# Four attention units ahead of the chunks instead of eight, queries of the last eight units turned on VectorE, and a stacked low-rank product

## Chip, cores and metric

One core of one Trainium2 chip runs the whole program in one launch. The metric is the device time in microseconds (us) of an execution; lower is better. The engines are TensorE (PE), VectorE (DVE), ScalarE (ACT), GpSimd (POOL) and SyncE (SP), which here only issues DMAs.

## What is computed

An attention in two steps feeds a gated channel mixer, which feeds a low-rank token mixer with a second two-layer channel mixer. All arrays are fp32.

```python
p_packed = sm_attn(p, k, v)            # 8 batches x 8 heads, 32 packed queries, 576 tokens, 64 dims
x = sm_attn(q, p_packed, p_packed)     # -> (8, 576, 512)
xk, xr = mu_k*x + (1-mu_k)*x_prev, mu_r*x + (1-mu_r)*x_prev
x = sigmoid(xr @ w_r) * (relu(xk @ w_k)**2 @ w_v)          # w_r 512x512, w_k 512x1024, w_v 1024x512
u = x + (x.transpose(0,2,1) @ U @ V).transpose(0,2,1)      # rank 32, U 576x32, V 32x576
out = u + relu(u @ w_ch1) @ w_ch2                          # 512x2048, 2048x512
```

## The kernel before, in words

**Plan and order.** Nothing is issued where it is written. Each helper of `Plan` records an operation with its tiles, and `emit` (L341) then plays the program with a small cost model (delays between engines `LAT`, a DMA that costs SP 60 ns, 500 ns of gap, its bytes at a fixed rate and 1700 ns to land) and takes, engine by engine, the ready operation with the lowest class `cls` and the lowest number. What comes out is one fixed order for each engine, so a different cost in the model is a different program. All DMAs go out from SP, but for the `wb` loads of phase 2, which go out from POOL.

**Attention** (`attention_steps`, L648). 16 units, one for each pair of batches (bp = 0..3) and pair of heads (j = 0..3). A unit loads `kin`, `qin`, `vin`, turns k and q on PE against an identity (`psat<-ident,qin`, nine 128x128 transposes in three groups, then copies out of PSUM into `qt`), makes the packed keys, and writes `xo` to `x_d` in HBM. Units 0 to 7 are "plain" (fp32 products without splitting, `NPLAIN`); 8 to 15 use split operands. Before, units 0 to 7 run as the **lead** (`NLEAD = 2*NJ`) on four sets of buffers (`A0`, B, C, D), each used twice.

**Weights.** `Cast` (L866) loads fp32 rows into `st` tiles and splits them into a high and a low fp32r part with four TENSOR_SCALAR and three SCALAR_TENSOR_TENSOR instructions on DVE. w_r and half of w_k are cast in the lead, the other twelve (`LATER`: all of w_v and the second half of w_k) once the lanes' buffers are free, in `cast_late` (L1003).

**Chunks.** Twelve chunks of 384 tokens, three for each pair of batches. A chunk loads x (`load_x`, L1043), mixes it with its shifted self, and runs `r_block` (psr, 36 matmuls of 512 columns), `k_block` (psk, 96 of 384), `v_block` (psv, 72 of 512), `x2_out` and `xu_block` (psu). Before, chunks 0 and 1 run interleaved, with x, r and kk of both in `A0`'s buffers (`x_lead`, `r_lead`, `kk_lead`, `xin_lead`). The attention of units 8 to 15 is laid between the chunks from chunk 2 on, `w_ch1` and `w_ch2` are split and stored to HBM from chunk 2, and `make_ws` (L1208) builds the weight sums of phase 2 in chunks 10 and 11.

**Phase 2.** Nine quarters of 512 tokens, eight f steps each: `product` (L1319) makes the seven products of a Strassen step (`psc<-ob,wb`, 256 columns), `c2_block` (L1342) the second layer (`psc<-w,hid`, 512 columns). The next quarter's u is loaded (`load_u`, L1252), gets the low-rank term (`h_block`, L1260: two matmuls psh for each tile of 128 tokens, since `vst` holds a high and a low part padded with zeros) and is turned (`t_block`).

Of the kernel before, what the change touches and what calls it, by code (L numbers as in the profile page):

```python
# [100 lines left out]
class Plan:  # L101
# [234 lines left out]
    TICK = 10240.0 / 3.0  # L336

# [3 lines left out]
    def emit(self):  # L341
# [27 lines left out]
        def release(op):  # L369
            def ready_on(e):  # L370
                return max([p.fin + self.lag(p.eng, e) for p in op.preds], default=0.0)
# [37 lines left out]
        while True:  # L409
# [46 lines left out]
            if op.cost == "dma":  # L456
                clock[e] = t + (60.0 if e == "sp" else 1000.0)
                dge = max(dge, t + 60.0) + 500.0
                wire = max(wire, dge + 700.0) + dur
                op.fin = wire + 1700.0  # L460
            else:
# [9 lines left out]
                clock[e] = t + dur  # L471
# [6 lines left out]
def packed_attention_moe_mixer_kernel(  # L478
# [31 lines left out]
    LANES, ORDER = "BCD", (0, 1, 2, 3, 0, 1, 2, 3)  # L510
# [66 lines left out]
    class Bufs:  # L577
# [24 lines left out]
        def tile_in(self, tag):  # L602
            return plan.tile(self.big_p, [P, 1152], F32, "big", parts=(0, 1, 2, 3), name=tag)
# [44 lines left out]
    def attention_steps(A, u, u_next):  # L648
# [69 lines left out]
        for c in range(3):  # L718
            yield
            ps = ps_att()  # L720
            for t in range(3):
                i = 3 * c + t
                plan.transpose(ps[:, t * P:(t + 1) * P], qin[:, i * P:(i + 1) * P], ident)
            n = 3 if c < 2 or not plain else 2
            w = 8 if plain else NI
            plan.copy(
                qt[:, 0:w * P].rearrange("p (b i c) -> p i b c", b=2, i=w)[:, 3 * c:3 * c + n],
                ps[:, 0:n * P].rearrange("p (i c b) -> p i b c", i=n, b=2))
            if c == 2 and plain:
# [194 lines left out]
    es_w1, es_att, es_x, es_st = ExitStack(), ExitStack(), ExitStack(), ExitStack()  # L924
# [7 lines left out]
    cv = Cast(es_att, "right")  # L932
# [4 lines left out]
    lane = [AX_[i] for i in ORDER]  # L937
    nxt = {}
    for u in range(NLEAD):
        nxt[u] = next((w for w in range(u + 1, NLEAD) if lane[w] is lane[u]), None)  # L940

# [10 lines left out]
    for what in FIRST.split():  # L952
# [8 lines left out]
        else:  # L961
            {"k": lane[u].load_k, "q": lane[u].load_q, "v": lane[u].load_v}[what[0]](u, go)
# [7 lines left out]
    steps = [attention_steps(lane[u], u, nxt[u]) for u in range(NLEAD)]  # L970
    prev = {w: u for u, w in nxt.items()}
    step = 0
    while any(s is not None for s in steps):
        if steps[NJ - 1] is None:
            att_banks[0] = banks[0:3] + banks[5:8]
        for i, s in enumerate(steps):
            if s is None or step < i * LAG or (i in prev and steps[prev[i]] is not None):
                continue
            if next(s, False) is False:
# [4 lines left out]
    rs = [plan.tile(A0.big_p, [P, 1152], F32, "big", parts=(0, 1), name="rs") for _ in range(3)]  # L984
    r_lead = [t.at(h)[:, h * 512:(h + 1) * 512] for t in rs for h in range(2)]
    pairs = [plan.tile(A0.big_p, [P, 1152], F32R, "big", parts=(0, 1), name="prs")[:, 0:2 * CW]
             .rearrange("p (a c) -> p a c", a=2) for _ in range(5)]
    x_lead, kk_lead = pairs[0:2], pairs[2:5]
    xin_lead = [t.vt.bitcast(F32)[:, 0:1024].rearrange("p (j c) -> p j c", j=2) for t in kk_lead[1:3]]
# [53 lines left out]
    def load_x(n):  # L1043
        b, c = chunks[n]
        if n == 1:
            for h, t in enumerate(xin_lead):
                plan.dma(t, x_d[b].rearrange("(j p) n -> p j n", p=P)[:, 2 * h:2 * h + 2, c * CW - P:c * CW + CW], cls=0)
            xin[n] = lambda j: xin_lead[j // 2][:, j % 2]
            return
# [25 lines left out]
    def r_block(n, t):  # L1075
# [7 lines left out]
        r = r_lead.pop(0) if r_lead else plan.tile(r_p, [P, 512], F32, "r")  # L1083
# [7 lines left out]
    def k_block(n, m):  # L1091
# [11 lines left out]
        if n < 2 and (2 * m + n) % 6 < 3:  # L1103
            kk = kk_lead[(2 * m + n) % 3]
        else:
            kk = plan.tile(kk_p, [P, 2, CW], F32R, "kk", parts=(0, 1))
# [3 lines left out]
    def v_block(n, m):  # L1110
        if m == 0:
            vps[n] = [plan.bank(banks[5 + t:6 + t] if n == 1 else ps_v, "psv", n != 1) for t in range(3)]
# [41 lines left out]
    vx_p, st_p, u_p, wb_p, w2r_p, tr_p = rpools = [Pool(bufs=n) for n in (1, 5, 4, 11, 1, 3)]  # L1154

    def open_r():
        es_att.close()
        for n, pl in zip("vx st2 u wb w2r tr".split(), rpools):
# [12 lines left out]
    c2_tags = [(home[t], t) for t in ["wk2_1", "wk3_1"] + [f"wv{m}" for m in range(MK)]]  # L1171
    c2_tags += [(w2r_p, "c2_0"), (w2r_p, "c2_1"), (xs_p, "xs")]
# [17 lines left out]
    def make_v():  # L1190
        vst = plan.tile(vx_p, [P, 2, NI, 2, 64], F32R, "vst", parts=(0, 1))
        vst_.append(vst)
        for c in range(2):
# [3 lines left out]
            for i0, i1 in ((0, 5), (5, NI)):  # L1197
                s = plan.tile(st_p, [P, 512], F32, "s", name="s_v")
                sv = s[:, 0:(i1 - i0) * 64].rearrange("p (i b c) -> p i b c", b=2, c=32)
                plan.zero(sv)  # L1200
                for g in range(4):
                    gr = slice(g * 32, (g + 1) * 32)
                    plan.copy(sv[gr, :, g % 2, :],
# [363 lines left out]
```

## Time and profile before

| | |
|---|---|
| median of 3 runs (lowest to highest) | 1488.79 us (1486.19 to 1491.61) |
| the profiled execution: its time, its span | 1491.34 us, 1489.6 us |
| granted TensorE clock, mean | 0.983 of 2.4 GHz |
| PE busy | 1461.4 us, 98% |
| PE weight loads (beside PE) | 1277.7 us, 86% |
| DVE busy | 980.2 us, 66% |
| ACT busy | 728.3 us, 49% |
| POOL busy | 270.3 us, 18% |
| chain that ended last | PE 92%, DMA 3%, DVE 2%, SP's queue 1% |
| HBM read, written | 229.84 MB, 60.89 MB |

The stages follow each other in time: the lead up to about 92 us, where the first psr stands, chunks up to about 700 us, and phase 2 behind that. Busy shares are means over all three. A matmul's duration in the rows overlaps that of the next one, so what a matmul holds PE for is read from one start to the next.

### The profile page before, as it was taken

What the parts mean: (1) busy time and instruction counts of PE and PEld (TensorE: products, weight loads), DVE (VectorE), ACT (ScalarE), POOL (GpSimd) and SP (SyncE); (2) the same over time, 40 slices, a digit from 0 to 9 for tenths busy, and PEclk for the clock granted to TensorE, in tenths of its full rate; (3) what the DMA queues carried; (4) which work ended last, traced back from release to release, by engine and by line L of the source; (5) the groups of instructions that cost most, each with busy time, mean ns of one, the idle gap of its engine ahead of it and who ended that gap; (6) DMA issues with size and microseconds to landing.
All of it is one profiled execution on the core that took longest, in us unless ns stands there. A gap on an engine that the chain in (4) does not pass through costs nothing.

```text
span 1489.6 us, 25587 instructions
## 1 busy us (share of the span) xinstructions
PE 1461.4 (98%) x9208; PEld 1277.7 (86%) x9208; DVE 980.2 (66%) x2143; ACT 728.3 (49%) x1534; POOL 270.3 (18%) x522
## 2 busy tenths in 40 slices
PE   6999999999999999999999999999999999999998
PEld 5667888888888888889899999899999999999997
DVE  6677877788888888786855464545555555554533
ACT  5567656666666666676533233323333332333332
POOL 0000000000000000001333333333333333333331
PEclk9689999999999999999999999999999999999999
DMA  8863335654655446666988888888888878878763
GB/s 233 234 175 121 114 101 137 205 182 136 186 179 156 141 141 218 207 226 191 314 228 237 211 208 245 198 244 229 231 212 229 213 201 239 213 216 222 206 176 99
DMA packets 213708, 292.42 MB, mean 196 GB/s; under 512 B 70224, under 2 KB 105360, under 8 KB 213584
## 3 DMA queue, kind: packets, MB, share of 16 engines
q1 hardware_dynamic: 141008, 158.65, 34.7%
q0 software_dynamic: 72576, 132.15, 34.0%
q8 instruction: 74, 1.21, 0.3%
q14 instruction: 50, 0.41, 0.1%
HBM read 229.84 MB, written 60.89 MB: 195 GB/s over the span
## 4 chain that ended last, share of the span: by engine, by line
PE 92%; DMA 3%; DVE 2%; SPq 1%; ACT 1%; issue 1%; DVEq 0%
PE psc L197 50%; PE psk L197 13%; PE psv L197 12%; PE psr L197 7%; PE psat L197 5%; PE psat L209 3%; SPq L319 1%; PE psh L197 1%; PE psu L197 1%; DMA kin<-in_k_dram 1%; DMA s<-w_d 1%; DMA qin<-in_q_dram 0%; DMA x_d<-xo 0%; DMA prs<-x_d 0%; DVE ob L254 0%
## 5 line engine op out<-in xcount | busy, mean ns | idle before, releaser
L197 PE MATMUL psc<-w,hid 128*128 128x512 f32 x1728 | 420.7, 391 | 0.2 <-ACT xu L288 0.2
L197 PEld LDWEIGHTS psc<-ob,wb 128*128 128x128 f32 x3024 | 386.4, 191 | 15.1 <-ACT tmp L288 0.8
L197 PE MATMUL psc<-ob,wb 128*128 128x256 f32 x3024 | 391.1, 282 | 0.4 <-ACT tmp L288 0.4
L319 POOL DMA_DIRECT2D wb<-ws_d x504 | 267.3, 530 | 565.5 <-PE psc L197 436.9
L197 PEld LDWEIGHTS psc<-w,hid 128*128 128x128 f32 x1728 | 314.9, 188 | 60.7 <-DVE hid L273 0.7
L233 ACT ACTIVATE hid<-tmp 128x256 fp32r<-128x256 f32 x216 | 131.6, 676 | 229.8 <-DVE tmp L254 229.8
L197 PE MATMUL psk<-xk,wk 128*128 128x384 f32 x1056 | 208.4, 340 | 1.3 <-ACT sq L233 0.8
L197 PE MATMUL psv<-wv,kk 128*128 128x512 f32 x783 | 202.0, 395 | 0.0
L197 PEld LDWEIGHTS psk<-xk,wk 128*128 128x128 f32 x1056 | 184.6, 188 | 10.6 <-issue 1.5
L197 PEld LDWEIGHTS psv<-wv,kk 128*128 128x128 f32 x783 | 144.2, 188 | 28.3 <-issue 0.8
L273 DVE SCALAR_TENSOR_TENSOR hid<-tmp,hid 128x256 fp32r<-128x256 f32 x216 | 126.5, 631 | 49.8 <-ACT hid L233 48.3
L254 DVE TENSOR_TENSOR tmp<-tmp,psc 128x256 f32<-128x256 f32 x288 | 113.1, 410 | 64.4 <-PE psc L197 64.1
L273 DVE SCALAR_TENSOR_TENSOR hid<-psc,hid 128x256 fp32r<-128x256 f32 x72 | 45.3, 629 | 166.5 <-ACT hid L233 166.5
L233 ACT ACTIVATE hid<-psc 128x256 fp32r<-128x256 f32 x72 | 45.9, 637 | 147.9 <-PE psc L197 147.5
L197 PE MATMUL psr<-wr,xr 128*128 128x512 f32 x414 | 112.3, 404 | 0.1
L311 POOL MEMSET x<- 128x8 f32 x4 | 0.5, 113 | 538.4 <-DVE m L270 538.1
L197 PEld LDWEIGHTS psr<-wr,xr 128*128 128x128 f32 x414 | 75.8, 190 | 18.4 <-issue 3.2
L288 ACT ACTIVATE tmp<-psc 128x256 f32<-128x256 f32 x144 | 56.5, 392 | 54.1 <-PE psc L197 53.5
L233 ACT ACTIVATE sq<-psk 128x384 f32<-128x384 f32 x96 | 46.5, 490 | 66.0 <-PE psk L197 63.6
L254 DVE TENSOR_TENSOR kk<-sq,kk 128x384 fp32r<-128x384 f32 x87 | 47.8, 552 | 32.0 <-ACT kk L288 31.8
L270 DVE SCALAR_TENSOR_TENSOR m<-x,mu_t,m 128x384 f32<-128x384 f32 x88 | 51.6, 610 | 0.9 <-ACT m L233 0.9
L233 ACT ACTIVATE m<-x,om_t 128x384 f32<-128x384 f32 x88 | 50.8, 607 | 2.5 <-DVE xr L254 1.8
(176 smaller groups left out, 1645.9 us busy)
## 6 DMA issues: line engine op xcount, KB each, us to landing
wb<-ws_d POOLq DMA_DIRECT2D x504, 256.0 KB, 3.7
st<-in_moe_w_ch_dram SPq DMA_DIRECT2D x32, 512.0 KB, 5.3
ws_d<-wb SPq DMA_DIRECT2D x56, 256.0 KB, 3.0
qin<-in_q_dram SPq DMA_DIRECT2D x32, 288.0 KB, 5.7
x_d<-xo SPq DMA_DIRECT2D x16, 576.0 KB, 3.4
x_d<-x SPq DMA_DIRECT2D x36, 256.0 KB, 2.2
u<-x_d SPq DMA_DIRECT2D x36, 256.0 KB, 5.2
out_dram<-u SPq DMA_DIRECT2D x36, 256.0 KB, 3.2
```

The costliest lines, as they stand in the source:

```text
L197: self.nc.tensor.matmul(o, l, r, start=start, stop=stop, **k)
L209: self.nc.tensor.transpose(out.get(), in_.get(), ident.get())
L233: self.nc.scalar.activation(o, in_.get(), func, **k)
L254: return self.elem(engs, lambda e, o, x, y: e.tensor_tensor(out=o, in0=x, in1=y, op=op), out, [a, b], self.TT, cls)
L270: ("dve",), lambda e, o, x, y, z: e.scalar_tensor_tensor(out=o, in0=x, scalar=z, in1=y, op0=op0, op1=op1), out, [a, b, s], {"dve": (1.042, ...
L273: ("dve",), lambda e, o, x, y: e.scalar_tensor_tensor(out=o, in0=x, scalar=s, in1=y, op0=op0, op1=op1), out, [a, b], self.TT, cls)
L288: self.nc.scalar.activation(o, i, AF.Copy)
L311: (self.nc.gpsimd if eng == "pool" else self.nc.vector).memset(o, 0.0)
L319: (self.nc.sync if eng == "sp" else self.nc.gpsimd).dma_start(out=o, in_=i)
```

## The change

Four things at once, and the planner's model beside them.

- **Lead and chunks.** `NLEAD = NJ`: units 0 to 3 run ahead, one for each set of buffers. The chunks go one by one from 0, and the attention of the next pair of batches (units 4 to 7, then 8 to 11, then 12 to 15) is laid over the three chunks of the pair before.
- **Queries of units 8 to 15** come in by eight DMAs of 32 partitions, with runs of 32 elements, and are turned in 32x32 blocks by two STREAM_TRANSPOSE instructions on DVE (`plan.turn`) instead of nine PE transposes and copies.
- **Conversion buffers** stay open behind the casts and become homes of three `w2` tiles and of `u` tiles; `make_ws` runs in chunks 7 to 10, all of `w_ch1` is cast ahead of `w_ch2`.
- **Low-rank product.** `vst` has no padding, X is stacked by batch, and a tile takes one psh matmul (two for the ninth). For this, u and the output move in halves of 64 rows, and xu in pieces of 32 rows.
- **Planner.** DMA costs have two settings, and DVE and ACT instructions that follow one another early in the program are taken to overlap.

```diff
+    AHEAD = 110000.0
+    CHUNKS = 500000.0
+    OVER = {"act": 100.0, "dve": 83.0}
+    LEAD = (60.0, 500.0, 1.0, 1700.0)
+    LOADED = (300.0, 100.0, 1.19, 3000.0)
...
-                clock[e] = t + (60.0 if e == "sp" else 1000.0)
-                dge = max(dge, t + 60.0) + 500.0
-                wire = max(wire, dge + 700.0) + dur
-                op.fin = wire + 1700.0
+                issue, gap, share, land = self.LEAD if t < self.CHUNKS else self.LOADED
+                clock[e] = t + (issue if e == "sp" else 1000.0)
+                dge = max(dge, t + issue) + gap
+                wire = max(wire, dge + 700.0) + dur * share
+                op.fin = wire + land
...
-    NLEAD = 2 * NJ
+    NLEAD = NJ
-    NPLAIN = 8
+    NPLAIN = 2 * NJ
...
+            if u >= NPLAIN:
+                for b2 in range(2):
+                    for h in range(2):
+                        src = q[2 * bp + b2, 2 * j + h].rearrange("(r t) (e s) -> e r t s", t=2 * NI, e=2)
+                        for e in range(2):
+                            g = 2 * h + e
+                            plan.dma(t.at(2 * g + b2)[g * 32:(g + 1) * 32, b2 * S:(b2 + 1) * S]
+                                     .rearrange("p (t s) -> p t s", s=32), src[e], after=after)
+                return
...
-        for c in range(3):
+        for c in range(3 if plain else 0):
...
+        if not plain:
+            yield
+            for b2 in range(2):
+                r = slice(b2 * S, (b2 + 1) * S)
+                plan.turn(qt[:, r].rearrange("p (i r e) -> p e i r", i=NI, e=2), qin[:, r])
...
-    steps = [attention_steps(lane[u], u, nxt[u]) for u in range(NLEAD)]
+    steps = [attention_steps(AX_[u], u, NJ if u == 0 else None) for u in range(NLEAD)]
...
-    for n in range(2, len(chunks)):
+    for n in range(len(chunks)):
         b, c = chunks[n]
-        if c == 2 and b + 2 < NBP:
+        if c == 0 and b + 1 < NBP:
             plan.cls = 1 if b == 0 else 0
-            for u in range((b + 2) * NJ, (b + 3) * NJ):
+            for u in range((b + 1) * NJ, (b + 2) * NJ):
                 attention(A0, u, u + 1 if u + 1 < NU else None)
...
-        for a in range(2):
-            plan.mm(ps, vst_[0].at(a)[:, a, i].rearrange("p b c -> p (b c)"), xt[b], start=(a == 0), stop=(a == 1))
+        if t < NI - 1:
+            k2 = t % 4
+            plan.mm(ps, vst_[0][:, 2 * k2:2 * k2 + 2].rearrange("p e c -> p (e c)"), xt[b, t // 4],
+                    start=True, stop=True)
+        else:
+            for b2 in range(2):
+                plan.mm(ps, vst_[0][:, NI - 1 + 2 * b2:NI + 1 + 2 * b2].rearrange("p e c -> p (e c)"), xt[b, b2],
+                        start=(b2 == 0), stop=(b2 == 1))
...
-                plan.dma(dst[:, i, :], u)
+                for to, i, rows in hs:
+                    plan.dma(dst[rows, i, :], u[to])
```

Over the whole program PE goes from 8562 to 8458 instructions (72 q transposes and 32 psh matmuls fewer), DVE from 2145 to 2134, ACT stays at 1472, POOL goes from 527 to 524, and SP from 623 to 782 (u and out from 36 each to 68, q from 32 to 80, xu pieces from 16 to 64).

SP's queue in the second half of the lead, before and now. `kin_261`, `qin_262` and `vin_326` are unit 4's (set `A0`), `kin_755` is the second unit of another set, `x_d0_65<-xo` the store of a finished unit, `x_233<-x_d0_65` a piece of chunk 0's x, and `st` a weight to be cast.

```order
L319 DMA x_d0_65<-xo_445 128x1152
L319 DMA st_725<-in_moe_w_k_dram 128x1024
L319 DMA kin_755<-in_k_dram 128x2x256 x2
L319 DMA kin_755<-in_k_dram 64x2x64 x2
L319 DMA x_233<-x_d0_65 128x384
L319 DMA x_233<-x_d0_65 128x2x63
L319 DMA st_815<-in_moe_w_k_dram 128x1024
L319 DMA kin_261<-in_k_dram 128x2x256 x2
L319 DMA kin_261<-in_k_dram 64x2x64 x2
L319 DMA qin_262<-in_q_dram 64x18x64 x2
```

```order
L319 DMA x_d0_65<-xo_448 128x1152
L319 DMA st_705<-in_moe_w_k_dram 128x1024
L319 DMA st_797<-in_moe_w_k_dram 128x1024
L319 DMA kin_261<-in_k_dram 128x2x256 x2
L319 DMA kin_261<-in_k_dram 64x2x64 x2
L319 DMA qin_262<-in_q_dram 64x18x64 x2
L319 DMA vin_326<-in_v_dram 128x2x256
L319 DMA vin_326<-in_v_dram 64x2x64
L319 DMA vin_326<-in_v_dram 128x2x256
L319 DMA vin_326<-in_v_dram 64x2x64
```

Before, the second units of all four sets are loaded here (`kin_755` is one of them); now unit 4 alone is, and the pieces of x and of weights that stood among those loads move up.

PE around unit 4's q transposes (`qin_262`) and the first psr, before and now; `th`, `pp` and `a2` belong to other units.

```order
L209 MATMUL psat_918<-ident_118,a2_662 128x128 x4
L209 MATMUL psat_919<-ident_118,a2_662 128x128
L209 MATMUL psat_924<-ident_118,qin_262 128x128 x3
L197 MATMUL psat_938<-kh_446,pT_216 32x256 x4
L197 MATMUL psat_938<-at_499,pT_216 32x64 x2
L197 MATMUL psat_945<-vin_244,at_794 32x64 x20
L209 MATMUL psat_986<-ident_118,qin_262 128x128 x2
L197 MATMUL psat_989<-th_663,pp_224 128x320
```

```order
L209 MATMUL psat_1036<-ident_118,a2_916 128x128 x4
L209 MATMUL psat_1037<-ident_118,a2_916 128x128
L197 MATMUL psat_1053<-th_917,pp_230 128x320
L197 MATMUL psat_1054<-th_917,pp_230 128x320
L197 MATMUL psat_1055<-th_917,pp_230 128x256
L197 MATMUL psat_1056<-th_917,pp_230 128x256
L197 MATMUL psr_1061<-wr0_200,xr_235 128x512 x3
L197 MATMUL psr_1061<-wr1_201,xr_236 128x512 x2
L209 MATMUL psat_1134<-ident_118,qin_262 128x128 x3
```

Unit 4's q stood ahead of steps of other lead units, which waited behind it, and now stands behind the first five psr matmuls of chunk 0.

The q of unit 8: on PE before, among psv and psk matmuls; on DVE now, among the mixing of a later chunk.

```order
L197 MATMUL psv_2688<-wv2_1874,kk_2561 128x512
L209 MATMUL psat_2839<-ident_118,qin_2675 128x128 x3
L197 MATMUL psv_2688<-wv2_1874,kk_2561 128x512 x2
L197 MATMUL psk_2780<-xk_2395,wk0_1_1875 128x384 x2
L209 MATMUL psat_2852<-ident_118,qin_2675 128x128 x3
L209 MATMUL psat_2858<-ident_118,qin_2675 128x128 x3
L197 MATMUL psk_2780<-xk_2395,wk0_1_1875 128x384
```

```order
L254 TENSOR_TENSOR xr_2394<-m_2476,xr_2394 128x384
L215 STREAM_TRANSPOSE qt_2505<-qin_2404 128x2x288
L277 TENSOR_REDUCE s2_2236<-psat_2488 128x16
L215 STREAM_TRANSPOSE qt_2505<-qin_2404 128x2x288
L277 TENSOR_REDUCE s2_2236<-psat_2489 128x4
L254 TENSOR_TENSOR xr_2406<-m_2477,xr_2406 128x384
```

Nine transposes in two or three pieces leave PE, and two instructions join DVE's order.

## Rows read from the trace of the kernel before

**Rows 1.** The page: span, PE's granted clock and DMA share in 40 slices.
```profile
span 1489.6 us, 25587 instructions
...
PEclk9689999999999999999999999999999999999999
DMA  8863335654655446666988888888888878878763
```
**Rows 2.** Windows by stage: window and length in us; busy us (instructions) of PE, PEld, DVE, ACT, POOL; clock; DMA share; GB/s.
```profile
35.00:92.00 57.00, 51.46 (x408) 36.06 (x409) 39.31 (x99) 31.93 (x90) 0.00 (x0) 0.67 0.84 239
...
220.00:520.00 300.00, 298.12 (x2037) 253.49 (x2036) 248.79 (x552) 204.00 (x439) 0.11 (x1) 1.00 0.55 166
520.00:700.00 180.00, 180.00 (x888) 160.21 (x887) 140.20 (x318) 118.10 (x247) 7.38 (x16) 1.00 0.63 204
800.00:1400.00 600.00, 600.00 (x3745) 542.46 (x3744) 326.41 (x676) 200.30 (x381) 207.80 (x392) 1.00 0.83 221
```
**Rows 3.** Waits of PE: engine, line, releaser: us in total, times, longest.
```profile
PE psat L209 <- DMA kin<-in_k_dram: 8.7, 5, 3.6
```
**Rows 4.** Timeline of PE in the lead: start, us, instruction, count, [idle before <-releaser].
```profile
55.77 2.12 PE L209 MATMUL psat<-ident,kin 128*128 128x128 f32 x10
...
63.61 0.52 PE L209 MATMUL psat<-ident,qin 128*128 128x128 f32 x3 [1.44 <-DMA qin<-in_q_dram]
...
87.65 0.31 PE L197 MATMUL psat<-vin,at 128*32 128x64 f32 x4
...
91.70 0.79 PE L197 MATMUL psr<-wr,xr 128*128 128x512 f32 x1
```
**Rows 5.** Timeline of PE at q transposes of a late unit.
```profile
352.94 1.22 PE L197 MATMUL psk<-xk,wk 128*128 128x384 f32 x6
354.00 0.49 PE L209 MATMUL psat<-ident,qin 128*128 128x128 f32 x3
354.24 0.60 PE L197 MATMUL psk<-xk,wk 128*128 128x384 f32 x2
354.68 0.49 PE L209 MATMUL psat<-ident,qin 128*128 128x128 f32 x3
```
**Rows 6.** Timeline of PE at a low-rank matmul.
```profile
715.35 0.39 PE L197 MATMUL psh<-X,vst 128*128 128x512 f32 x1
715.58 0.39 PE L197 MATMUL psu<-xs,ust 128*128 128x512 f32 x1
```
**Rows 7.** Windows of the lead and of chunks 0 and 1 (columns as rows 2).
```profile
3.00:100.00 97.00, 82.48 (x672) 58.59 (x672) 66.75 (x168) 54.96 (x158) 0.00 (x0) 0.75 0.87 241
...
48.00:140.00 92.00, 83.81 (x719) 60.38 (x719) 69.47 (x172) 61.96 (x167) 0.00 (x0) 0.84 0.62 183
92.00:220.00 128.00, 123.95 (x799) 102.84 (x799) 100.72 (x228) 86.44 (x194) 0.11 (x1) 0.99 0.34 106
160.00:200.00 40.00, 39.14 (x199) 35.27 (x198) 37.80 (x85) 24.96 (x49) 0.00 (x0) 1.00 0.31 100
```
**Rows 8.** Timeline of SP where it loads the last piece of x ahead of the chunks.
```profile
95.86 3.81 SPq L319 DMA_DIRECT2D x<-x_d  x4
```
**Rows 9.** Groups by form: operation, count | busy us, mean ns | idle before, releaser.
```profile
L288 ACT ACTIVATE qt<-psat 128x384 f32<-128x384 f32 x27 | 13.1, 489 | 5.2 <-PE psat L209 4.6
...
L215 DVE STREAM_TRANSPOSE qt<-a 128x576 f32<-128x576 f32 x8 | 6.2, 772 | 0.0
...
L254 DVE TENSOR_TENSOR xa<-xa,xb 128x512 f32<-128x512 f32 x4 | 2.7, 682 | 0.0
```
**Rows 10.** Timeline of SP: loads of a late unit.
```profile
229.91 2.37 SPq L319 DMA_DIRECT2D kin<-in_k_dram  x4
232.32 2.27 SPq L319 DMA_DIRECT2D qin<-in_q_dram  x2
```
**Rows 11.** DMA issues on the page: count, KB each, median us from issue to landing.
```profile
qin<-in_q_dram SPq DMA_DIRECT2D x32, 288.0 KB, 5.7
```
**Rows 12.** Timeline of SP at the end: the last stores.
```profile
1484.37 2.22 SPq L319 DMA_DIRECT2D out_dram<-u  x4
```

More of the change, by code (lines that the diff above doesn't have):

```diff
@@ L921, in split @@
         plan.tt(lo, src, hi, sub, engs)
-    es_w1, es_att, es_x, es_st = ExitStack(), ExitStack(), ExitStack(), ExitStack()
+    es_w1, es_cv, es_att, es_x, es_st = [ExitStack() for _ in range(5)]
     w1a = Pool(obj=open_pool(es_w1, "w1a", 1, "left"))
@@ L969, in packed_attention_moe_mixer_kernel @@
     A0.after = go
-    steps = [attention_steps(lane[u], u, nxt[u]) for u in range(NLEAD)]
-    prev = {w: u for u, w in nxt.items()}
+    steps = [attention_steps(AX_[u], u, NJ if u == 0 else None) for u in range(NLEAD)]
     step = 0
     while any(s is not None for s in steps):
-        if steps[NJ - 1] is None:
-            att_banks[0] = banks[0:3] + banks[5:8]
         for i, s in enumerate(steps):
-            if s is None or step < i * LAG or (i in prev and steps[prev[i]] is not None):
-                continue
-            if next(s, False) is False:
+            if s is not None and step >= i * LAG and next(s, False) is False:
                 steps[i] = None
@@ L1111, in v_block @@
         if m == 0:
-            vps[n] = [plan.bank(banks[5 + t:6 + t] if n == 1 else ps_v, "psv", n != 1) for t in range(3)]
+            vps[n] = [plan.bank(ps_v, "psv") for t in range(3)]
         kk = kk_t.pop((n, m))
@@ new lines, in halves_of, with load_u @@
+    def halves_of(T):
+        b, t = divmod(T, NI)
+        if t == NI - 1:
+            return b, [(slice(0, P), t, slice(0, P))]
+        b2, k2 = divmod(t, 4)
+        return b, [(slice(e * 64, (e + 1) * 64), 2 * k2 + e, slice(b2 * 64, (b2 + 1) * 64)) for e in range(2)]
+    def load_u(T, after=()):
+        b, hs = halves_of(T)
+        pl, tag = (((cv.tp, "a"), (cv.tp, "m")) * 2 + ((r_p, "r"),) * 3 + ((x2_p, "x2"),) * 3)[T % 10]
+        u_t[T] = plan.tile(pl, [P, DM], F32, tag, name="u", parts=(0, 1))
+        for n, (to, i, rows) in enumerate(hs):
+            t = u_t[T].at(n) if len(hs) > 1 else u_t[T]
+            plan.dma(t[to], x2_d[b].at(i)[rows, i * DM:(i + 1) * DM], after=after)
@@ L1373, in packed_attention_moe_mixer_kernel @@
         casts.append((slice(0, P), w_ch1[:, m * P:(m + 1) * P], 512, put1))
+    for m in range(MC):
         def put2(w, m=m):
@@ L1420, in packed_attention_moe_mixer_kernel @@
             evac.append(r_block(n, t))
-            if t == 0 and n == 2:
-                for n0 in range(2):
-                    v_block(n0, MK - 1)
-                x2s = [(n0, t0, x2_out(n0, t0)) for t0 in range(3) for n0 in range(2)]
-            elif t == 0:
+            if t == 0 and n > 0:
                 x2s = finish(n - 1)
@@ L1450, in packed_attention_moe_mixer_kernel @@
             plan.cls = 1
-            if n == NCAST:
-                opened_r = plan.open(rpools, A0.pools + cv.pools, open_r)
-        if n > NCAST:
+        if n == FIRST_WS - 1:
+            opened_r = plan.open(rpools, A0.pools, open_r)
+        if FIRST_WS <= n < FIRST_WS + 4:
             plan.cls = 3
-            for f in range(NF // 2):
-                make_ws((n - NCAST - 1) * (NF // 2) + f)
+            for f in range(2):
+                make_ws(2 * (n - FIRST_WS) + f)
             plan.cls = 1
-        if n == NCAST + 1:
+        if n == len(chunks) - 2:
             make_v()
@@ L1463, in packed_attention_moe_mixer_kernel @@
             prep0 = [f for T in range(4) for f in (lambda T=T: h_block(T), lambda T=T: t_block(T))]
-        if n == NCAST + 2:
+        if n == len(chunks) - 1:
             operands(0)
-            for m in range(2):
+            for m in range(3):
                 load_w2(m)
@@ L1479, in packed_attention_moe_mixer_kernel @@
             T0 = 4 * q + 4
-            for T in range(T0, T0 + 4):
-                load_u(T)
+            if q > 0:
+                for T in range(T0, T0 + 4):
+                    load_u(T)
             hs = [[lambda T=T: h_block(T)] for T in range(T0, T0 + 4)]
```

145 lines of the change are left out of this document (52 added, 93 removed).

## The prediction

> **What bounds the kernel now.** I read the page first, then windows by stage, then what PE waits for, and last the timelines at the places that the change touches. The page gives the span, 1489.6 us, and the granted clock over its 40 slices: only the first three slices (some 112 us) are not at the full level [rows 1]. By stage PE is never free behind them: 298.12 of 300 us busy in the middle chunks, 180.00 of 180 in the last ones, 600.00 of 600 in phase 2, all at a clock of 1.00 [rows 2]. So behind the lead the time is the sum of what PE is given, and a matmul that goes away is worth its place in PE's row. The lead is another matter. Between 35 and 92 us PE's clock is granted at 0.67, the DMA engines are 84% busy at 239 GB/s, and DVE is busy for 39.31 of 57 us [rows 2]. PE's largest wait is there, for kin, 8.7 us in five waits [rows 3]; unit 4's first q transpose comes behind an idle of 1.44 us for its load [rows 4].
>
> The sum is made against the profiled execution, 1491.3 us (1489.6 of span and 1.7 around it), which stands 2.5 above the median of 1488.8.
>
> **The q transposes of units 8 to 15.** 72 transposes leave PE, in 24 groups of three. A group starts at 354.00 and the next matmul at 354.24, so it holds PE for 0.24 us [rows 5]. Two psk matmuls between two groups take 0.44 us (354.24 to 354.68), six take 1.06 (352.94 to 354.00), so 0.18 each, 0.35 for two, and the change of kind costs the other 0.09 [rows 5]. 24 x 0.24 = **-5.8 us**. The changes of kind stay: in the listing PE alternates between attention and chunk matmuls 261 times before and 263 times now, since the pieces of units 4 to 7 now lie between chunk matmuls. 2 x 0.09 = +0.2, which I leave out. On the other side stand 16 STREAM_TRANSPOSE on DVE. The nearest form takes 772 ns [rows 9], together 12.4 us, and the 24 copies out of PSUM that go were 489 ns on ACT [rows 9] or a little more on DVE. DVE is busy for 248.79 of 300 us there [rows 2]: 12.4 us over 480 us of chunks raises that share of 83% by 2.6 points at most. Nothing, as long as a unit has a chunk's time of slack; if that cover is gone, a turn that is late holds up all of PE by its own 0.77 us, 16 times, 12 us.
>
> **The low-rank product.** 72 psh matmuls become 40. One holds PE from 715.35 to 715.58, 0.23 us [rows 6]. 32 x 0.23 = **-7.4 us**. They lie among psc matmuls at a full clock, where nothing hides them. The price is on other engines: eight more additions and subtractions for X of the kind that takes 682 ns [rows 9], 5.5 us of DVE in phase 2, where it is busy for 326.41 of 600 us [rows 2]: nothing. SP issues 32 more u pieces, 32 more out pieces and 48 more xu pieces; at the 0.55 us of an out store (2.22 us for four) [rows 12] that is 62 us of an SP queue in 790 us, with the wb loads on POOL's: nothing but at the very end. There the last tiles go out in two halves: one more issue behind the last sum, **+0.5 us**.
>
> **Lead and chunks.** The sum of the plain attention work stays; it moves. Four gains are bounded by rows. The first psr stands at 91.70 [rows 4]. Of what PE does between 55.77 and 87.65 for the second units of the lanes [rows 4], unit 4's first steps stay ahead of it and units 5 to 7 do not; 19 pieces of the timeline, the first kin at 55.77 and the last at 87.65, some 16.6 us of PE, belong to units 4 to 6, of which 3.3 stay, so chunk 0 could start at 91.7 - 13.3 = 78.4. The loads allow it: SP issues the last x of chunk 0 at 95.86 to 99.67 [rows 8] and counted by bytes in both listings 4.2 MB fewer stand ahead of it now, at 241 GB/s [rows 7] 17 us. So a gain of up to **13 us**.
>
> What takes it back is DVE. Before, twelve late weight casts had two interleaved chunks of PE work beside them; now chunk 0 alone must have them, since its v_block needs all of w_v. In the order, the last instruction of the last w_v cast is the 295th on DVE (365th before) and chunk 0's first xr stands at about the 145th, so 150 instructions lie between. At a mean of 100.72/228 = 0.442 us [rows 7] they are 66 us of work. From 78.4 on, at DVE's share in the window from 160 to 200 us, 37.80/40 = 94.5% [rows 7], they are done at 148. At its share from 48 to 140 us, 69.47/92 = 75.5% [rows 7], at 166. And where is PE before at the same work? 5.5 units and 204 chunk matmuls now stand against 8 units and some 102 before, both about 83 us of work on PE, which it has behind it at 148 us before. So at a DVE that is kept fed the lead comes out at **0**, at the slower share 18 us later; and if DVE is not in the way at all, 13 us earlier. I take 0: the casts are a queue of ready work, as from 160 to 200 us, and not a lead that waits for loads; both ends go into the range.
>
> A rule of the pages speaks on the gain's side. The row shows PE at a clock of 0.67 while it is 90% busy with attention steps, and at 0.99 behind the first psr [rows 2, 7]. The Trainium skill, TensorE: Matmul & The Clock Gate, Part 4, says that transposes on PE do not count as activity for the clock in the way that matmuls do. The trace agrees as far as it goes: the stretch at 0.67 is the one full of transposes. By that rule an earlier chunk 0 lifts the clock earlier too, which is part of the first rival below.
>
> Planner and homes: w2 tiles, u tiles and make_ws move to other places of an order in which PE has no idle time [rows 2]. Their waits aren't in this trace; from below they are worth nothing, as there is no idle time to win, and from above an SP load in the wrong place costs its 5.7 us to land [rows 11] once or twice. I take 0.
>
> **Sum.** -5.8 - 7.4 + 0.5 + 0 = -12.7: 1478.6 for an execution like the profiled one, 1476.1 at its distance to the median. I forecast **1476 us**. About 0.3%, 4.5 us, is what a measurement of this kernel can tell from no change.
>
> **Rivals.**
> *The early start goes through.* DVE keeps up with the twelve casts, because chunk 0's mixes are few and unit 4 to 7's work on DVE is spread over three chunks. Then -13 stands: 1476 - 13 = **1463**. For: DVE reaches 94.5% once [rows 7]. Against: 66 us of DVE work in a queue whose PE side is shorter than that.
>
> *The first chunk starves.* DVE runs at the share of the window from 48 to 140 us, 75.5%, because its casts wait for weights behind unit 4's loads or for their one set of buffers; w_v is done at 166 and not at 148. PE waits in v_block of chunk 0 with everything behind it: +18, **1494**, and at 70% (172) +24, 1500. It decides from a DVE share below 80% (161, +13) between the first psr and the last w_v cast. For: the share in that very window before. Against: there DVE had its own loads to wait for.
>
> *SP's queue.* A q load is eight issues in place of two, with runs of 128 bytes in place of 256. Before, qin's two issues took 2.27 us and kin's four 2.37 [rows 10], so eight take between 8 x 0.59 = 4.7 and 8 x 1.14 = 9.1, 2.5 to 6.9 us more. In the order three of these loads stand right ahead of a chunk's x. If x is late by that, with 3.7 taken, 3 x 3.7 = 11 us: **1487**, no change that can be measured. Against: SP has slack at 55% to 63% of the DMA engines [rows 2]. The Trainium skill, DMA: Bandwidth & Descriptors, Specifications, puts full rate at transfers of 512 bytes and up, and its Rules for kernel authors advise against splitting a transfer into partition halves, as this change does for u and out. The trace agrees in part: qin takes 5.7 us to land [rows 11] at 288 KB. Phase 2's halves keep rows of 2 KB, where the DMA engines are 83% busy [rows 2]; a slowdown there would come as PE waiting for u or for wb, and would give the same 1487 or so.
>
> That the change doesn't do what it says is excluded for PE: the listing has 104 matmuls and transposes fewer.
>
> **How the numbers follow.** Forecast 0.46, within 1468 to 1484. Early start 0.24. SP's queue 0.18. Starved first chunk 0.12. Faster by over 0.3% means under 1484.3: forecast and early start, 0.46 + 0.24 = 0.70. Within: 0.18. Slower, above 1493.3: 0.12. The range reaches from a bit below the early start to the starved chunk at its own price, 1460 to 1495.
>
> **What would show it.** PE instructions 104 fewer, PE's busy time lower by some 13 us; psh x40. PE's idle behind 220 us still under 1%. The first psr at 76 to 82 us: if it is still near 92, the loads and not unit 4 to 7 set it. DVE's share between it and the last wk_1 or w_v cast above 90%: right; below 80% with PE waiting for `wv` in chunk 0: the second rival. PE waiting for DMA x at the starts of chunks 3 to 6: the third. The forecast is wrong in kind if phase 2 shows waits for wb or w2, which I priced at nothing.

## The result, and the profile after

The change takes 1471.72 us (median of five runs, 1469.25 to 1473.45) against 1489.73 us (five runs): a ratio of 0.9879 with a 95% interval of 0.9861 to 0.9898, 18.0 us less. The forecast was 1476.0, in a range of 1460 to 1495. The profiled execution took 1469.25 us with a span of 1467.5, which is 22.1 us under the profiled one of before; of the two, this one is the fastest of its five and that one stands 1.6 us above its median, so the pair shows 4.1 us more than the medians do. They differ in TensorE's clock too: the profiled execution of before has a mean granted clock of 0.983, where the 63 executions of it that were timed beside the experiments stand at 0.983 to 0.995 (median 0.991), and the five of the change stand at 0.985 to 0.990.

The page of the change: span, PE's line, and the clock and DMA share over 40 slices, as in [rows 1].

```profile
span 1467.5 us, 25589 instructions
...
PE 1433.9 (98%) x9104; PEld 1256.9 (86%) x9104; DVE 984.9 (67%) x2132; ACT 722.8 (49%) x1534; POOL 269.3 (18%) x519
...
PEclk8889999999999999999999999999999999999999
DMA  8864444655555777920999998899998889779763
```

PE has 104 instructions fewer, as the listing said (9208 before), and 27.5 us less busy time (1461.4 before). That is more than the 13 us of the removed matmuls. Part of the rest lies in the lead: from 35 to 92 us PE is busy for 51.46 us before [rows 2] and for 43.83 now, at a granted clock of 0.67 and 0.85 in these two executions.

The windows of the change, those of [rows 2] first and then those of [rows 7]:

```profile
35.00:92.00 57.00, 43.83 (x383) 32.88 (x384) 53.97 (x130) 40.12 (x107) 0.00 (x0) 0.85 0.83 238
...
220.00:520.00 300.00, 296.97 (x1963) 251.40 (x1962) 253.89 (x558) 206.63 (x456) 0.32 (x2) 1.00 0.59 176
520.00:700.00 180.00, 179.77 (x903) 160.02 (x901) 140.54 (x295) 113.07 (x234) 9.24 (x18) 1.00 0.57 182
800.00:1400.00 600.00, 600.00 (x3750) 542.82 (x3749) 328.26 (x685) 196.56 (x381) 208.51 (x394) 1.00 0.88 224
...
48.00:140.00 92.00, 81.03 (x559) 65.74 (x559) 88.28 (x209) 69.67 (x163) 0.00 (x0) 0.91 0.64 192
92.00:220.00 128.00, 128.00 (x876) 106.56 (x875) 97.92 (x224) 89.30 (x196) 0.11 (x1) 1.00 0.47 134
```

From 48 to 140 us DVE is busy for 88.28 of 92 us, 96%, where it was 75.5% [rows 7]. From 92 to 220 us PE is never idle at all. Behind 220 us PE was full and is full: it is idle for 3.3 us from 220 to 700 us (1.9 before) and for none from 800 to 1400.

Where the 22.1 us went can be read from the products of phase 2, which both kernels hold in equal number. The rows give count, durations, and the start of the first and the last one. Before:

```profile
L197 PE MATMUL psc<-ob,wb x3024: 274/283/386, 708.0 to 1480.9; 128*128 128x256 f32 x189
...
L197 PE MATMUL psc<-w,hid x1728: 387/389/500, 714.4 to 1485.1; 128*128 128x512 f32 x192
```

And with the change:

```profile
L197 PE MATMUL psc<-ob,wb x3024: 274/283/287, 691.5 to 1456.7; 128*128 128x256 f32 x189
...
L197 PE MATMUL psc<-w,hid x1728: 387/389/497, 698.1 to 1460.9; 128*128 128x512 f32 x192
```

Phase 2 begins 16.5 us earlier (708.0 to 691.5). From its first product to its last it takes 769.4 in place of 777.1 us, 7.7 less; 28 of the 32 psh matmuls that went stood there, the other four ahead of it. From the last product to the end of the span it takes 6.6 in place of 4.5, 2.1 more. -16.5 - 7.7 + 2.1 = -22.1. If the q transposes are worth the forecast's 5.8 of the first part and the four psh 0.9, some 10 us are left for the lead, to which the forecast gave nothing. Of the 18.0 us of the medians some 6 are left in the same way.

The start of chunk 0 on PE, which answers to [rows 4] (timeline: start, us, instruction, count, [idle before <-releaser]):

```profile
68.47 1.33 PE L209 MATMUL psat<-ident,a 128*128 128x128 f32 x5 [4.23 <-DVE a L254]
70.46 2.38 PE L197 MATMUL psat<-th,pp 64*128 64x320 f32 x8 [0.66 <-DVE th L291]
72.78 2.41 PE L197 MATMUL psr<-wr,xr 128*128 128x512 f32 x5
75.06 0.55 PE L209 MATMUL psat<-ident,qin 128*128 128x128 f32 x3
```

The first psr stands at 72.78 us, 18.9 earlier and 5.6 before the forecast's 78.4. The idle ahead of it is now DVE's doing: 4.23 us for one `a`, in a stretch where DVE is 53.97 of 57 us busy.

### The profile page after: what moved, and what is told of

Its sections match the earlier page's. It is cut to its first block, busy times and chain, and to the rows that moved or that the text cites. A ratio compares the mean times of both kernels' runs of the same rounds, so it can differ in the third digit from the quotient of the medians.

```text
span 1467.5 us, 25589 instructions
## 1 busy us (share of the span) xinstructions
PE 1433.9 (98%) x9104; PEld 1256.9 (86%) x9104; DVE 984.9 (67%) x2132; ACT 722.8 (49%) x1534; POOL 269.3 (18%) x519
## 4 chain that ended last, share of the span: by engine, by line
PE 91%; DMA 3%; DVE 2%; ACT 1%; SPq 1%; issue 0%; DVEq 0%; ACTq 0%
PE psc L197 52%; PE psk L197 13%; PE psv L197 13%; PE psr L197 7%; PE psat L197 3%; PE psat L209 2%; DMA st<-in_moe_w_k_dram 1%; PE psu L197 1%; SPq L319 1%; ACT a L233 1%; DMA w_d<-m 1%; PE psh L197 1%; DMA st<-in_moe_w_v_dram 0%; DMA st<-in_moe_w_r_dram 0%; DMA st<-in_moe_w_ch_dram 0%
## 5 line engine op out<-in xcount | busy, mean ns | idle before, releaser
L197 PE MATMUL psk<-xk,wk 128*128 128x384 f32 x1152 | 228.0, 341 | 0.2 <-ACT sq L233 0.2
L197 PE MATMUL psv<-wv,kk 128*128 128x512 f32 x864 | 224.7, 396 | 0.0
L197 PEld LDWEIGHTS psk<-xk,wk 128*128 128x128 f32 x1152 | 201.1, 188 | 11.2 <-issue 3.7
L197 PEld LDWEIGHTS psv<-wv,kk 128*128 128x128 f32 x864 | 158.6, 188 | 32.2 <-issue 2.3
L197 PEld LDWEIGHTS psr<-wr,xr 128*128 128x128 f32 x432 | 81.7, 193 | 20.7 <-DVE xr L291 1.5
L254 DVE TENSOR_TENSOR kk<-sq,kk 128x384 fp32r<-128x384 f32 x96 | 52.8, 552 | 33.2 <-ACT kk L288 32.4
L233 ACT ACTIVATE m<-x,om_t 128x384 f32<-128x384 f32 x96 | 55.0, 606 | 4.0 <-DVE xr L254 3.8
L270 DVE SCALAR_TENSOR_TENSOR m<-x,mu_t,m 128x384 f32<-128x384 f32 x96 | 56.4, 609 | 0.7 <-ACT m L233 0.4
```

The costliest lines, as they stand in the source:

```text
L197: self.nc.tensor.matmul(o, l, r, start=start, stop=stop, **k)
L233: self.nc.scalar.activation(o, in_.get(), func, **k)
L254: return self.elem(engs, lambda e, o, x, y: e.tensor_tensor(out=o, in0=x, in1=y, op=op), out, [a, b], self.TT, cls)
L270: ("dve",), lambda e, o, x, y, z: e.scalar_tensor_tensor(out=o, in0=x, scalar=z, in1=y, op0=op0, op1=op1), out, [a, b, s], {"dve": (1.042, ...
```

## The experiments

Each kernel was timed in rounds with the kernel before on the same chip. The change itself stands at a ratio of 0.9879; 0.0034 of ratio are 5 us. The kernel before had a median of 1486.92 to 1489.73 in the different sets, so a difference of medians across them is uncertain by some 3 us; where it matters, both ways of reckoning are given.

### Undoing the two parts of the forecast's sum

**The q transposes back on PE.**

```diff
-            if u >= NPLAIN:
+            if u >= NU:
...
-        for c in range(3 if plain else 0):
+        for c in range(3):
...
-        if not plain:
-            yield
-            for b2 in range(2):
-                r = slice(b2 * S, (b2 + 1) * S)
-                plan.turn(qt[:, r].rearrange("p (i r e) -> p e i r", i=NI, e=2), qin[:, r])
```

> The changed kernel with the q of units 8 to 15 loaded in two pieces and turned on PE as before (nine transposes and three copies a unit). Theory A, the price of the forecast: 24 groups hold PE for 0.24 us each, so 5 to 8 us slower than the change (1477 to 1480). Rival B, the eight small loads and the turns on DVE cost what the transposes saved: within 2 us of the change. Rival C, a late turn had held up PE: faster than the change.

Measured: 1478.13 us, ratio 0.9938 (0.9923 to 0.9953). By the medians 6.4 us slower than the change, by the ratios 8.8. Theory A stands; rivals B and C fall. The trace says where. From the first psr of chunk 3 to the first product of phase 2 the change takes 439.2 us (252.3 to 691.5) and this run 443.3 (252.6 to 695.9), 4.1 more, with 63 of the 72 transposes, 5.1 us by the forecast's price. Of the 8.9 us between the two profiled executions most of the rest lies in phase 2, where no q is turned:

```profile
L197 PE MATMUL psc<-ob,wb x3024: 274/283/415, 695.9 to 1465.6; 128*128 128x256 f32 x189
...
L197 PE MATMUL psc<-w,hid x1728: 387/389/504, 702.5 to 1469.8; 128*128 128x512 f32 x192
```

That is 773.9 us in place of 769.4, with 2.3 us of waits of PE for `hid`. So 6.4 us is not the price of the transposes alone; some of it is the order that the planner made anew.

**32 low-rank matmuls added again**, as products by the zeros that `vst` holds.

```diff
-                    start=True, stop=True)
+                    start=True, stop=False)
+            plan.mm(ps, vst_[0][:, NI:NI + 2].rearrange("p e c -> p (e c)"), xt[b, t // 4],
+                    start=False, stop=True)
```

> The changed kernel with a second low-rank matmul, by zeros, for 32 of the 36 tiles, as many psh matmuls as before (72). Theory A: each holds PE for 0.23 us that nothing hides, so 7.4 us slower than the change (1479). Rival B: phase 2 has slack that takes them in, under 3 us.

Measured: 1476.86 us, ratio 0.9934 (0.9917 to 0.9951), 5.1 us slower by the medians and 8.2 by the ratios. The trace says it more sharply. In phase 2 of this run the products stand so:

```profile
L197 PE MATMUL psc<-ob,wb x3024: 274/283/353, 695.8 to 1468.2; 128*128 128x256 f32 x189
...
L197 PE MATMUL psc<-w,hid x1728: 387/389/504, 702.5 to 1472.4; 128*128 128x512 f32 x192
```

695.8 to 1472.4 is 776.6 us, 7.2 more than the 769.4 of the change and half a microsecond from the 777.1 of before. 28 of the 32 stand in this stretch: 6.6 us without a wait of PE of 0.6, or 0.24 us for each, with nothing in phase 2 that hides them. Theory A stands.

**Both undone**, which leaves the lead, the planner and the homes.

> The changed kernel with both of these undone: what is left is the lead of four units, the chunks one by one, the planner and the homes. Theory A, the earlier start goes through: first psr at 71 to 79 us, DVE over 93% busy from 48 to 140 us, the time 5 to 10 us under the kernel before (1480 to 1485). Rival B, the forecast's own step (the twelve casts on DVE give the earlier start back): within 2 us of the kernel before, 1488 to 1491, with PE waiting on wv in chunk 0.

Measured: 1481.03 us, ratio 0.9957 (0.9942 to 0.9973), 6.4 us under the kernel before. The first psr is at 72.1 us, and the window that the expectation names shows DVE at 88.73 of 92 us, 96%:

```profile
48.00:140.00 92.00, 83.30 (x561) 67.79 (x561) 88.73 (x209) 69.59 (x162) 0.00 (x0) 0.87 0.64 190
92.00:220.00 128.00, 128.00 (x875) 106.80 (x874) 97.21 (x220) 89.37 (x195) 0.11 (x1) 1.00 0.47 136
```

In its profiled execution phase 2 begins at 696.9, 11.1 us before the 708.0 of the kernel before, whose profiled execution lies above its median. By the medians the gain is 6.4 to 6.7 us, with the end in it, where this kernel too has 6.6 us behind its last product for the 4.5 of before: 8.5 to 8.8 without the end. From chunk 3 to phase 2 it takes 444.3 us, 5.1 more than the change. So the lead does gain, with both other parts gone, and the step that gave it nothing was wrong. Theory A stands. The planner's second DMA setting and the homes are still in this kernel; what the first of them is worth comes last.

### What makes the lead's gain

**The planner's overlap off.**

```diff
-    AHEAD = 110000.0
+    AHEAD = 0.0
```

> The changed kernel with the planner's overlap of DVE and ACT instructions off (AHEAD = 0), the rest as it is. Theory A, fewer units ahead of chunk 0 make the gain, not the model: within 3 us of the change. Rival B, the overlap in the model is what keeps DVE fed: DVE's share from 48 to 140 us falls under 90%, first psr later than 78 us, 5 to 10 us slower than the change.

Measured: 1487.16 us, ratio 1.0004 (0.9989 to 1.0018). It has the change's fewer units in the lead, its 104 instructions fewer on PE, and no gain: 15.4 us slower than the change. It still holds the low-rank product and the turns of q, some 10 us net of the end (7.7 and 4 to 5 less, 2.1 more), so its early start doesn't merely give nothing: it loses about 10 us against the kernel before. Rival B stands, with more than it asked for. The windows of this run, and PE's waits between 93 and 165 us:

```profile
48.00:140.00 92.00, 82.29 (x544) 63.96 (x543) 78.53 (x189) 65.91 (x157) 0.00 (x0) 0.83 0.64 188
140.00:160.00 20.00, 13.59 (x60) 9.70 (x59) 16.76 (x39) 9.34 (x20) 0.00 (x0) 0.83 0.23 68
```

```profile
PE psat L209 <- DVE a L254: 3.4, 1, 3.4
PE psv L197 <- ACT wv L288: 2.4, 1, 2.4
PE psr L197 <- DVE xr L254: 0.6, 1, 0.6
```

DVE is at 78.53/92 = 85%, and from 140 to 160 us PE is idle for 6.4 us, for w_v among others. In the change the same window reads:

```profile
140.00:160.00 20.00, 20.00 (x126) 15.80 (x125) 14.65 (x33) 15.92 (x36) 0.00 (x0) 1.00 0.77 206
```

This is the prediction's rival of the starved first chunk, at the place that it named and at some 10 us of its 18. Between the first psr and the last DVE instruction of the last w_v cast the two runs show, the change first:

```profile
72.80:137.60 64.80, 61.89 (x402) 51.11 (x402) 63.32 (x149) 51.31 (x114) 0.00 (x0) 0.93 0.57 166
```

```profile
77.80:156.00 78.20, 69.26 (x429) 55.56 (x429) 71.32 (x167) 55.66 (x124) 0.00 (x0) 0.91 0.50 145
```

Without the overlap the first psr is 5.0 us later, 18 more DVE instructions stand ahead of the last cast (167 for 149), and DVE is at 91% in place of 98%. Together that is 18.4 us at the last cast.

**The overlap alone, on the kernel before.**

```diff
+    AHEAD = 110000.0
+    OVER = {"act": 100.0, "dve": 83.0}
...
-                clock[e] = t + dur
+                clock[e] = t + (max(dur - self.OVER.get(e, 0.0), 0.0) if t < self.AHEAD else dur)
```

> The kernel before with nothing but the planner's overlap of DVE and ACT instructions (AHEAD, OVER) added. Theory A, the overlap is a gain by itself, wherever DVE and ACT feed PE: 8 to 16 us faster than before, PE's first psr earlier than 88 us, DVE's share from 48 to 140 us over 85%. Theory B, it only decides with one chunk at a time, where the twelve casts have little beside them: within 4 us of before.

Measured: 1485.07 us, ratio 0.9988 (0.9975 to 1.0002), 1.9 us under the kernel before by the medians of the same set. The first psr is at 83.0 and not 91.7, but DVE stays at 71.92 of 92 us, 78%, and little of the 9 us is left at the end. Theory B stands. The early start without the overlap loses some 10 us and the overlap without it gives next to nothing; the gain of the lead is where both are.

**The overlap for DVE alone.**

```diff
-    OVER = {"act": 100.0, "dve": 83.0}
+    OVER = {"dve": 83.0}
```

> The changed kernel with the planner's overlap for DVE alone (none for ACT). Theory A, DVE is the engine that chunk 0 waits for, so its overlap is what makes the order: within 4 us of the change. Rival B, ACT's counts as much: 8 us slower or more, near the run without both.

Measured: 1482.1 us, ratio 0.9965 (0.9949 to 0.9981), 10.4 us slower than the change. Its first psr is the earliest of all at 71.1 us, but 165 DVE instructions stand between it and the last w_v cast, at 146.1. Rival B stands: without ACT's entry 10.4 us are lost, without both 15.4, though DVE is the busier engine. A run with ACT's entry alone was not made.

**The overlap for longer.**

```diff
-    AHEAD = 110000.0
+    AHEAD = 500000.0
```

> The changed kernel with the planner's overlap reaching to 500 us of its own time in place of 110. Theory A, the overlap pays where DVE is the bound, which it is up to about 130 us: within 3 us of the change. Theory B, it pays all through the chunks, where DVE is 83% busy: 3 to 8 us faster. Theory C, it misplaces work where DVE waits for others: slower by over 3 us.

Measured: 1485.54 us, ratio 0.9986 (0.9976 to 0.9996), 13.8 us slower than the change, theory C. The lead is as in the change (first psr at 74.6, DVE 88.09 of 92 us); the loss is in the middle chunks:

```profile
220.00:520.00 300.00, 290.68 (x1917) 241.52 (x1916) 280.43 (x632) 204.33 (x451) 0.32 (x2) 1.00 0.67 208
```

DVE has 632 instructions there in place of 558, 93% of the window, and PE is idle for 9.3 us where it was for 3.0, most of all for `th` from ACT (4.2 us). The planner, which now believes DVE to be faster, moves later work up, above all the weight sums of phase 2 (28 of the additions `wb<-sums,wb` for 11). The idle time is 6.3 of the 13.8 us; where the rest goes isn't shown.

### How much slack chunk 0 has against DVE

**Twelve more DVE instructions, planned in.**

```diff
                 plan.ts(ab, ab, 0x1FF, None, ALU.bitwise_and)
+                if plan.cls == 1:
+                    plan.ts(ab, ab, 0x1FF, None, ALU.bitwise_and)
```

> The changed kernel with one TENSOR_SCALAR of the twelve late casts done twice (the second changes nothing), 12 more instructions of about 0.4 us on DVE, 5 us in all, in the stretch where DVE is over 95% busy. Theory A, DVE sets when chunk 0 and its v_block run: 4 to 6 us slower than the change. Rival B, PE's own order and the loads set it: under 2 us slower.

Measured: 1481.72 us, ratio 0.9968 (0.9955 to 0.9982), 10.0 us slower, well over the 4 to 6 of theory A. The windows of its profiled execution, which at 1484.62 us is 2.9 over its median, show a loss beyond the idle time:

```profile
140.00:145.00 5.00, 2.58 (x10) 1.35 (x8) 4.94 (x13) 3.00 (x6) 0.00 (x0) 1.00 0.00 0
145.00:150.00 5.00, 3.95 (x12) 1.95 (x12) 2.71 (x6) 2.20 (x6) 0.00 (x0) 0.72 0.43 113
150.00:155.00 5.00, 5.00 (x15) 3.46 (x15) 2.79 (x5) 1.83 (x4) 0.00 (x0) 0.50 0.74 264
155.00:160.00 5.00, 5.00 (x40) 3.52 (x39) 3.14 (x6) 1.84 (x6) 0.00 (x0) 0.76 0.73 227
```

PE is idle for 2.42 and 1.05 us, for an `xr`, an `a` and a `th`, not for w_v, and its clock is granted at 0.72, 0.50 and 0.76 in the last three. Estimated from these rows, 5 us each at these levels cost 1.4 + 2.5 + 1.2 = 5.1 us of full speed: here the clock takes more than the wait. A typical execution pays less: this one has a mean clock of 0.982, the other eleven 0.985 to 0.990.

**The same twelve, without the planner knowing.** The doubled instruction is issued inside the same operation, so the order of all engines stays that of the change.

> The changed kernel with the same doubled TENSOR_SCALAR in the twelve late casts, but the planner isn't told of it, so that every engine keeps the order of the change. At 0.42 us each less 0.08 of overlap that is 4 us more on DVE up to the last w_v cast. Theory A, PE has next to no slack against DVE at the end of chunk 0: an idle of PE near 140 to 150 us and 4 to 10 us slower than the change. Rival B, the 10 us of the run before came from the other order it was planned into: under 3 us slower.

Measured: 1474.25 us, ratio 0.9911 (0.9895 to 0.9928): 2.5 us slower by the medians, 4.8 by the ratios. The last w_v cast's last instruction on DVE stands at 141.1, 3.5 us later, and in the window from 140 to 160 us PE is idle for 0.7 us at a clock of 1.00:

```profile
140.00:160.00 20.00, 19.29 (x115) 14.21 (x114) 15.13 (x34) 14.58 (x28) 0.00 (x0) 1.00 0.54 163
```

This lies between the two theories. The idle time that A predicted is there, but small; so at least half of the 10 us of the run before came from the order that the planner chose with twelve instructions more, not from the 4 us of work. It is also the cleanest sight of the bound: in one and the same order, 3.5 us more at the last cast cost 2.5 to 4.8 us at the end.

**Twelve fewer, planned in.**

```diff
-                plan.ts(ab, ab, 0x1FF, None, ALU.bitwise_and)
+                if plan.cls != 1:
+                    plan.ts(ab, ab, 0x1FF, None, ALU.bitwise_and)
```

> The changed kernel without that TENSOR_SCALAR in the late casts (it leaves out the mask of the low part, so the low parts of w_v and half of w_k are other numbers), planned anew: 12 instructions, 4 us, less on DVE. Theory A, PE has no idle time left from 93 us on, so DVE's relief brings at most 3 us. Rival B, the time follows DVE's work in a line: 8 to 10 us faster than the change. If any new order costs: slower.

Measured: 1471.04 us, ratio 0.9887 (0.9868 to 0.9906), the same as the change. Theory A stands: from 140 to 160 us PE was full already, and less work on DVE has nothing more to give there.

**The late casts' copies on ACT alone.**

```diff
-                plan.copy(hi, m)
+                plan.copy(hi, m, ("act",) if plan.cls == 1 else ("act", "dve"))
```

> The changed kernel with the copies of the late casts' high parts on ACT alone (five of twelve are on DVE now), 2 us less on DVE and 3 more on ACT, planned anew. Theory A, nothing to win from 93 us on: within 3 us of the change. Rival B: over 3 us faster. A new order alone that costs: over 3 us slower, with an idle of PE near 140 to 160 us.

Measured: 1475.0 us, ratio 0.9916 (0.9897 to 0.9934), 3.3 us slower by the medians and 5.5 by the ratios. Theory A and rival B miss; the third case, a new order that costs, is what came. The last w_v cast comes when it did (137.4), but PE waits 1.6 us for an xr of chunk 1 and is idle for 2.7 us between 140 and 160.

### The planner's second DMA setting

```diff
-    CHUNKS = 500000.0
+    CHUNKS = 1e12
```

> The changed kernel with the planner's first DMA setting to the end (CHUNKS = 1e12). Theory A, phase 2 has no idle time on PE to win or lose by it: within 3 us of the change. Rival B, the second setting brings loads of u, w2 and wb early enough: PE waits for DMAs between 500 and 900 us, over 4 us slower than the change.

Measured: 1474.62 us, ratio 0.9915 (0.9898 to 0.9932), 2.9 us slower by the medians, 5.4 by the ratios: on the border of the two theories. In its profiled execution PE waits once between 690 and 800 us, where the change doesn't wait at all:

```profile
PE psc L197 <- DVE tmp L254: 2.3, 1, 2.3
```

PE names no DMA, but the engines that it waits for do. In the same window they wait for loads of w2:

```profile
ACT w L288 <- DMA s<-w_d: 7.2, 4, 4.2
```

```profile
DVE w L291 <- DMA s<-w_d: 3.7, 1, 3.7
```

In the change neither engine waits for `s<-w_d` there. From the first product of phase 2 to the last this run takes 774.8 us (692.9 to 1467.7), 5.4 more than the change. So rival B's mechanism is there, one step behind PE and for w2 alone; whether the second setting is worth 3 us or 5 the runs don't tell.

## Why the prediction was right, and the step that failed

**The low-rank product**: -7.4 forecast, -7.7 between the first and the last product of phase 2, where 28 of the 32 stood, and 7.2 back there when 32 matmuls by zero were added. Its cover was as said: PE is 600.00 of 600 us busy, and the eight more additions for X cost nothing that shows.

**The q transposes**: -5.8 forecast, 6.4 back (medians) when undone, of which 4.1 show in the chunks that hold them; in the kernel with both parts undone it is 5.1. The turn took what the nearest form did, 770 ns for 772:

```profile
L215 DVE STREAM_TRANSPOSE qt<-qin 128x576 f32<-128x576 f32 x16 | 12.3, 770 | 0.0
```

**The end**: +0.5 forecast, +2.1 measured. The change ends on seven stores that SP issues in a row:

```profile
1460.21 4.31 SPq L319 DMA_DIRECT2D out_dram<-u  x7
```

At 0.62 us each SP is 3.6 us behind the last product (1464.5 to 1460.9), where it was 1.5 behind with four. The term counted one more issue behind the last sum; three more in a row was the right count.

**The lead** is the step that failed: "So at a DVE that is kept fed the lead comes out at 0", from "150 instructions", "a mean of 100.72/228 = 0.442 us" and "94.5%". Each of its parts was a little too slow. The first psr came at 72.8 and not at 78.4. The 149 instructions took 63.32 us and not 66. DVE was at 98% and not at 94.5%. The last w_v cast's work on DVE thus stood at 137.6 us and not at 148, 10 us earlier, and the lead gave 6 to 9 us by the medians, some 10 to 11 in the profiled pair. The mechanism, that DVE's work up to the last cast sets how much of the early start is kept, is borne out: the same order with 3.5 us more on DVE lost 2.5 to 4.8 us, and in every variant of the change in which DVE's last cast came at 146 us or later, PE ran dry for 2.6 us or more between 140 and 160 us. It isn't the only thing: with the last cast at 137.4 (the copies on ACT) PE ran dry for 2.7 us as well. And it is w_v itself that PE waits for only where the overlap is off; elsewhere it is mixes and attention steps.

Behind this stands a part that was priced at nothing. The prediction spoke of the planner only for phase 2 ("Planner and homes ... I take 0"). The five constants were in the diff, and for the lead they were what decided: with AHEAD at 0 the first psr is at 77.8, nearly the 78.4 of the working, the last cast at 156.0, between its ends of 148 and 166, and the lead loses some 10 us. The working counted its 150 instructions in the new order, but took DVE's share and mean from the order that the same diff replaced.

That the measured time is only 4.3 us from the forecast is in part luck: the lead gave 6 to 9 us more, the end took 1.6 more, and the q transposes gave a little less.

**The rivals.** The early start went through in part: 6 to 9 of 13 us by the medians, so that the result lies between the forecast (1476) and this rival (1463), nearer the forecast. The starved first chunk is what the run without the overlap shows. SP's queue: the loads became longer as worked out, 5.33 to 6.05 us where the eight issues follow in a row, against 2.27 for two [rows 10], 3.1 to 3.8 more where 3.7 was taken, for example

```profile
249.83 6.05 SPq L319 DMA_DIRECT2D qin<-in_q_dram  x8
```

but PE waits for no x and no q behind 220 us. The loads are early enough to hide it. The Trainium skill, DMA: Bandwidth & Descriptors, Rules for kernel authors, advises one transfer of 128 partitions in place of two to disjoint halves. The trace agrees at the end, where nothing hides them: the halves of the output cost 2.1 us there, 1.6 more than forecast. That u's halves in phase 2 cost nothing is the other side: PE is full there. The row that the prediction took as agreement in part, 5.7 us for qin to land [rows 11], is no sign of its short runs: u, in rows of 2 KB, takes nearly as long on the same page of the profile of before.

```profile
u<-x_d SPq DMA_DIRECT2D x36, 256.0 KB, 5.2
```

The clock, which by the prediction an earlier chunk 0 would lift, went up in the profiled pair, 0.85 for 0.67 between 35 and 92 us. But the kernel before with the overlap alone, with the same transposes and its first psr at 83.0 us, shows 0.85 there as well:

```profile
35.00:92.00 57.00, 47.63 (x424) 32.74 (x426) 45.64 (x115) 34.62 (x101) 0.00 (x0) 0.85 0.94 258
```

And over all executions the mean clock of the kernel before (median 0.991 of 63) is not below that of the change (0.988 of five). That an earlier chunk 0 lifts the clock, as the prediction took from the Trainium skill's remark on transposes (TensorE: Matmul & The Clock Gate, Part 4), is not shown here, and 0.67 is no mark of the kernel before.

## What to carry to other kernels

If an order is made by a cost model and a change edits that model, the shares and waits of the old trace are no longer the ones to extrapolate from: list the order of the engine that feeds the bound one, and count what stands ahead of its last due instruction. Work that left a full PE came off the time at about its place in PE's row (7.4 forecast, 7.7 measured; 5.1 forecast for 63 transposes, 4.1 and 5.1 measured), so such terms can be trusted within a microsecond or so of the trace; the terms that need another engine to keep up can come out on either side, and the range has to hold both. Before a difference of two traces is read, look where each profiled execution stands among its fellows, in time and in clock. At the very end of a program count every store that is issued in the last row of them, not only the last.

## What was not expected of the hardware

In the run with twelve instructions more, idles of PE of 3.5 us in all, between 140 and 150 us in a stretch at full clock, were followed by the lower of its two levels, 1.2 of 2.4 GHz: it was granted at 0.72, 0.50 and 0.76 in the 15 us from 145 us on, by estimate another 5.1 us. In the same 20 us, idles of 0.7 us (the doubled instruction in the same order), 2.6 us (the overlap for DVE alone) and 2.7 us (the copies on ACT) left it at 1.00, so that no rule on the size of an idle comes out of these runs. And DVE's instructions begin before the one ahead has ended: in the change, from the first psr to the last w_v cast, 132 of 147 start 0.07 to 0.1 us before the end of the last, as here, a start at 135.27 against an end at 134.66 + 0.68 = 135.34:

```profile
134.66 0.68 DVE L273 SCALAR_TENSOR_TENSOR a<-a,st 128x512 f32<-128x512 int32 x1
135.27 0.80 DVE L277 TENSOR_REDUCE s<-a 128x20 f32<-128x640 f32 x1
```

The model's 83 ns for DVE says the same, and a planner that counts such durations end to end takes DVE for slower than it is: the change planned without the overlap is 15.4 us slower.
